# A recurrent attention kernel with a gated FFN: steps by halves of heads, the last eight tokens of each segment projected in advance, and an FFN at 512 tokens

## The chip, the cores and the metric

The kernel runs on one NeuronCore of a Trainium2 chip. The metric is the device time of one execution, in microseconds (us). The fast runs of one kernel lie within about 1% of each other. An experiment was timed against the kernel before on the same chip, in the same rounds. Over the different rounds the median of the kernel before went from 3629 to 3643 us, so differences of a few tens of microseconds between runs of different rounds are uncertain.

## The reference, cut to what matters

```python
# x: [2048, 1024]; 32 heads of 128; segments of 32 tokens; 8 memory tokens; FFN width 3584
mem = mem0                                          # [8, 1024]
for s in range(64):                                 # 64 steps, each needs the one before
    h = concatenate([mem, x[32*s : 32*s+32]])       # 40 rows
    q, k, v = h @ Wq, h @ Wk, h @ Wv                # each weight 1024 x 4096, bf16: 8 MB
    p = softmax(mask(q @ k.T * 128**-0.5))          # the memory rows see all 40, the others are causal
    o = (p @ v) @ Wo                                # Wo: 4096 x 1024, 8 MB
    mem = o[:8]
    outs.append(o[8:])
a = concatenate(outs)
b = (gelu(x @ w_gate) * (x @ w_up)) @ w_down        # FFN
g = sigmoid((x * gate_w).sum(-1, keepdims=True))
out = g * a + (1 - g) * b
```

The recurrence runs through `mem`. Each step needs all four attention weights, 32 MB together, which is more than fits in SBUF, the on-chip memory, here: about two thirds of it can stay. A step has only 40 rows to multiply, so it has little arithmetic per byte of weight.

## The kernel before

The weights are cut into 64 pieces of 512 KB ("pieces"). 41 stay in SBUF for all steps (tiles `res`). The other 23 are loaded again in every step through five buffers (tiles `ring`). SP issues these loads. The next load into a buffer is issued when PE has used the old content:

```python
streamed = [((p + 1) * NSTR) // 64 > (p * NSTR) // 64 for p in range(64)]
def load_str():
    ...
    p = str_pos[n % NSTR]
    t = ring[n % NRING]                                          # NRING = 5
    op("sp", lambda e: e.dma_start(dst(t, p), src(p)), wr=[t.r()], lane=f"ring{n % NRING}")
def consumed(s, p):
    if not streamed[p]:
        return
    ...
    load_str()
```

Semaphores are not written by hand. A helper notes for every operation what it reads and writes, and derives the waits. A transfer carries a `lane` and is asynchronous. If a write meets an earlier asynchronous write of the same region, the later one waits until the earlier one has landed:

```python
def _touch(self, op, reg, write, async_):
    ...
    if kind == "S":                       # SBUF: one key for each 64 bytes of a partition's offset
        keys = [("S", c) for c in range(reg[1] // CELL, (reg[2] + CELL - 1) // CELL)]
    else:
        keys = [reg]                      # any other tuple is its own key
    ...
    for k in keys:
        ...
        w, rd = c
        if write:
            if w is not None and (w.sem is not None or w.eng != op.eng or async_):
                deps.append(w)            # wait for the earlier writer
...
for o in ops:                             # emit(), per engine, in program order
    for s, v in o.waits:
        e.wait_ge(s, v)                   # the engine's sequencer stands here
    ins = o.fn(e)
```

An SBUF region is an offset and a length within a partition. The helper does not know which partitions are written.

In a step, 24 tokens of the segment and the 8 memory rows form one product of 32 rows. The last 8 tokens of a segment do not depend on memory. They are projected in every fourth step for four segments together (second input `xR`, which doubles the q, k and v products of that step). All heads are treated at once, so the softmax stands in series with the products:

```python
R = i == 0                                                 # i = s % 4
quad(s, "q", 0, *bq[0]); ...; quad(s, "k", 1, *bq[3])     # each quad: 8 pieces, one half of the heads
op("pe", f_sa, ...); op("pe", f_sb, ...); ...              # scores of all heads, both orientations
quad(s, "v", 0, *bv[0])
op("pe", f_d, ...)                                         # shift by the maximum
op("act", ... ACTF.Exp ...)
quad(s, "v", 1, *bv[1])
op("pe", f_den, ...)                                       # denominators
op("act", ... ACTF.Ln ...); op("dve", ...); op("act", ... ACTF.Exp ...)
op("pe", f_pva, ...)                                       # p @ v, needs all of the above
for g in range(4): ...                                     # copies to oT
for gp in range(4): ...                                    # 16 pieces of Wo, the first needs oT
...                                                        # result, transpose, new memory columns of hT
```

The FFN follows, at 256 tokens a time: w_down stays in SBUF, and the slabs of w_gate and w_up are loaded again for each of the eight groups, four slabs ahead.

## Time and profile before

| quantity | value |
|---|---|
| median of 3 runs | 3643.69 us (3643.08 to 3645.5) |
| span of the profiled run | 3637.2 us, mean granted clock 0.858 |
| one step, mean | 42.9 us |
| steps, all 64 | to about 2844 us |
| FFN | 793 us |

The first line of the profile's page gives each engine's busy time, its share of the span and its instruction count:

```profile
PE 2512.6 (69%) x44606; PEld 1401.3 (39%) x44678; DVE 800.5 (22%) x1873; ACT 565.3 (16%) x1315; POOL 115.9 (3%) x348
```

PE is the busiest engine, but 69% is an average over stages with different limits. The view by stretch separates them. Its columns are named in its first line; the stretches shown are the steps, two short stretches of one step, each just behind a softmax wait, and the FFN:

```profile
core 0: us, PE busy (x) PEld busy (x) DVE busy (x) ACT busy (x) POOL busy (x), PEclk, DMA share, GB/s
142.00:2802.00 2660.00, 1801.24 (x38522) 902.79 (x38522) 445.15 (x1023) 355.05 (x819) 96.45 (x248) 0.85 0.83 286
...
1062.00:1064.00 2.00, 2.00 (x55) 1.01 (x45) 0.78 (x3) 0.01 (x1) 0.00 (x0) 1.00 0.43 150
1074.00:1076.00 2.00, 2.00 (x56) 1.54 (x52) 0.00 (x0) 0.00 (x0) 0.00 (x0) 0.62 0.37 89
2899.00:3637.00 738.00, 609.94 (x4403) 445.16 (x4472) 322.49 (x731) 176.41 (x445) 0.00 (x0) 0.92 0.53 166
```

During the steps the DMA engines are busy for 0.83 of the time, PE for 1801 of 2660 us. In the two short stretches DMA falls to about 0.4 while PE is fully busy: PE had stood in a softmax wait just before, the ring had filled meanwhile, and nothing was left to load.

The timeline of PE shows both kinds of waiting. Columns are the start, the duration, engine and line, operation, output and inputs, shapes and count; brackets hold PE's idle time before it and what ended it:

```profile
1049.74 0.40 PE L496 MATMUL pb<-ring_90,hT_56 128*32 128x512 bf16 x4 [0.69 <-DMA ring_90<-in_A_Wq_dram]
1051.15 0.40 PE L496 MATMUL pb<-ring_91,hT_56 128*32 128x512 bf16 x4 [0.25 <-DMA ring_91<-in_A_Wk_dram]
1052.42 0.40 PE L496 MATMUL pb<-ring_92,hT_56 128*32 128x512 bf16 x4 [0.44 <-DMA ring_92<-in_A_Wk_dram]
1053.86 0.40 PE L496 MATMUL pb<-ring_93,hT_56 128*32 128x512 bf16 x4 [0.60 <-DMA ring_93<-in_A_Wk_dram]
...
1069.79 0.45 PE L692 MATMUL pb<-EA,vA 32*128 32x40 bf16 x32 [1.85 <-DVE vA L521]
...
1072.60 0.62 PE L727 MATMUL pb<-res_126,oT 128*32 128x256 bf16 x8 [2.12 <-DVE oT L710]
```

At first PE uses one streamed piece every 1.27 to 1.44 us and waits for each one: the loads bound this part. Later it waits 1.85 us for the copy of v and 2.12 us for the copies of the attention result: the serial chain bounds that part. The waits of PE over 1000 to 2000 us (total, times, longest) say the same of many steps:

```profile
PE pb L727 <- DVE oT L710: 36.1, 17, 2.1
PE pb L692 <- DVE vA L521: 33.3, 18, 1.9
PE pb L496 <- DMA xR<-xb_scr: 31.8, 6, 6.6
...
PE pb L496 <- DMA ring_90<-in_A_Wq_dram: 16.6, 16, 1.9
```

The third line is the special step that waits for `xR`.

### The profile page before, as it was taken

What the parts mean: (1) busy time and instruction counts of PE and PEld (TensorE: products, weight loads), DVE (VectorE), ACT (ScalarE), POOL (GpSimd) and SP (SyncE); (2) the same over time, 40 slices, a digit from 0 to 9 for tenths busy, and PEclk for the clock granted to TensorE, in tenths of its full rate; (3) what the DMA queues carried; (4) which work ended last, traced back from release to release, by engine and by line L of the source; (5) the groups of instructions that cost most, each with busy time, mean ns of one, the idle gap of its engine ahead of it and who ended that gap; (6) DMA issues with size and microseconds to landing.
All of it is one profiled execution on the core that took longest, in us unless ns stands there. A gap on an engine that the chain in (4) does not pass through costs nothing.

```text
span 3637.2 us, 95669 instructions
## 1 busy us (share of the span) xinstructions
PE 2512.6 (69%) x44606; PEld 1401.3 (39%) x44678; DVE 800.5 (22%) x1873; ACT 565.3 (16%) x1315; POOL 115.9 (3%) x348
## 2 busy tenths in 40 slices
PE   3667666666666666767676666766666488888887
PEld 2233333333323333333333333333332366666665
DVE  1111111111111111111111111111111144444444
ACT  2111111111111111111111111111111022222222
POOL 1000000000000000000000000000000000000000
PEclk9688888988888788878887988888888699999998
DMA  8987887888787978787887888787978655555554
GB/s 300 357 288 270 281 295 278 305 282 306 258 314 255 317 255 312 265 292 270 303 281 271 309 278 287 262 312 260 305 264 318 240 174 173 174 173 174 173 174 126
DMA packets 437038, 957.86 MB, mean 263 GB/s; under 512 B 51736, under 2 KB 178712, under 8 KB 436640
## 3 DMA queue, kind: packets, MB, share of 16 engines
q1 hardware_dynamic: 421280, 939.15, 75.1%
q10 hardware_dynamic: 15360, 12.59, 1.1%
q8 instruction: 349, 5.72, 0.6%
q14 instruction: 49, 0.40, 0.0%
HBM read 934.82 MB, written 16.78 MB: 262 GB/s over the span
## 4 chain that ended last, share of the span: by engine, by line
PE 44%; DMA 39%; DVE 7%; ACT 4%; issue 4%; SPq 1%; POOL 1%; ACTq 0%; POOLq 0%
PE pb L496 14%; PE pb L727 8%; PE pb L848 8%; PE pb L873 4%; DMA xR<-xb_scr 3%; DMA ring_91<-in_A_Wk_dram 3%; DMA ring_93<-in_A_Wk_dram 3%; DMA ring_92<-in_A_Wk_dram 3%; DMA ring_94<-in_A_Wk_dram 3%; PE pb L528 2%; DMA ring_90<-in_A_Wk_dram 2%; PE pb L733 2%; DMA ring_93<-in_A_Wq_dram 2%; DMA ring_91<-in_A_Wq_dram 2%; DMA ring_94<-in_A_Wq_dram 2%
## 5 line engine op out<-in xcount | busy, mean ns | idle before, releaser
L858 DVE SCALAR_TENSOR_TENSOR tp<-s_145,pb 128x256 f32<-128x256 f32 x224 | 94.2, 420 | 304.5 <-ACT s_145 L857 304.5
L848 PE MATMUL pb<-xT,rb_138 128*128 128x256 bf16 x896 | 124.7, 286 | 50.2 <-DMA rb_138<-in_B_w_gate_dram 50.2
L857 ACT ACTIVATE s_145<-pb 128x256 f32<-128x256 f32 x224 | 85.9, 383 | 452.8 <-PE pb L848 396.3
L848 PE MATMUL pb<-xT,rb_140 128*128 128x256 bf16 x896 | 122.6, 282 | 40.1 <-DMA rb_140<-in_B_w_gate_dram 40.1
L727 PE MATMUL pb<-res_126,oT 128*32 128x256 bf16 x512 | 42.4, 402 | 143.3 <-DVE oT L710 101.9
L848 PE MATMUL pb<-xT,rb_139 128*128 128x256 bf16 x896 | 122.0, 281 | 5.6 <-DMA rb_139<-in_B_w_up_dram 5.6
L848 PEld LDWEIGHTS pb<-xT,rb_138 128*128 128x128 bf16 x896 | 91.3, 102 | 88.5 <-DMA rb_138<-in_B_w_gate_dram 52.4
L848 PE MATMUL pb<-xT,rb_141 128*128 128x256 bf16 x896 | 120.4, 279 | 4.5 <-DMA rb_141<-in_B_w_up_dram 4.5
L675 DVE SCALAR_TENSOR_TENSOR pb<-pb,LN 128x320 f32<-128x320 f32 x64 | 31.9, 499 | 400.7 <-ACT LN L673 400.7
L848 PEld LDWEIGHTS pb<-xT,rb_140 128*128 128x128 bf16 x896 | 90.3, 101 | 77.2 <-DMA rb_140<-in_B_w_gate_dram 42.1
L861 DVE SCALAR_TENSOR_TENSOR g_147<-tp,pb 128x256 f32<-128x256 f32 x224 | 94.4, 422 | 108.9 <-ACT tp L860 108.9
L860 ACT ACTIVATE tp<-tp 128x256 f32<-128x256 f32 x224 | 93.2, 416 | 115.8 <-DVE tp L858 115.8
L692 PE MATMUL pb<-EA,vA 32*128 32x40 bf16 x2048 | 25.4, 183 | 123.8 <-DVE vA L521 88.8
L519 ACT ACTIVATE vA<-pb 128x512 bf16<-128x512 f32 x64 | 38.2, 597 | 424.1 <-PE pb L496 424.1
L848 PEld LDWEIGHTS pb<-xT,rb_139 128*128 128x128 bf16 x896 | 89.8, 101 | 20.4 <-DMA rb_139<-in_B_w_up_dram 8.0
L541 DVE COPY qT<-pb 128x1024 bf16<-128x1024 bf16 x64 | 44.3, 692 | 242.0 <-PE pb L528 242.0
L848 PEld LDWEIGHTS pb<-xT,rb_141 128*128 128x128 bf16 x896 | 89.2, 100 | 18.2 <-DMA rb_141<-in_B_w_up_dram 6.4
L541 DVE COPY kT<-pb 128x512 bf16<-128x512 bf16 (+1 forms) x112 | 51.7, 461 | 179.8 <-PE pb L528 179.8
L710 DVE CAST oT<-pb 128x320 bf16<-128x320 f32 x128 | 62.9, 492 | 121.4 <-ACT oT L708 121.4
L519 ACT ACTIVATE tok_71<-pb 128x512 bf16<-128x512 f32 x55 | 32.8, 597 | 320.0 <-PE pb L496 296.2
L873 PE MATMUL pb<-wd,GT_149 128*128 128x512 bf16 x273 | 73.2, 388 | 13.4 <-DVE GT_149 L863 11.6
L521 DVE CAST tok_72<-pb 128x512 bf16<-128x512 f32 x38 | 26.2, 690 | 251.5 <-PE pb L496 215.8
(408 smaller groups left out, 5138.2 us busy)
## 6 DMA issues: line engine op xcount, KB each, us to landing
ring_90<-in_A_Wk_dram SPq DMA_DIRECT2D x77, 512.0 KB, 6.2
ring_91<-in_A_Wk_dram SPq DMA_DIRECT2D x77, 512.0 KB, 6.4
ring_93<-in_A_Wk_dram SPq DMA_DIRECT2D x77, 512.0 KB, 6.1
ring_94<-in_A_Wk_dram SPq DMA_DIRECT2D x77, 512.0 KB, 6.3
ring_91<-in_A_Wv_dram SPq DMA_DIRECT2D x77, 512.0 KB, 6.5
ring_92<-in_A_Wv_dram SPq DMA_DIRECT2D x77, 512.0 KB, 6.4
ring_94<-in_A_Wv_dram SPq DMA_DIRECT2D x77, 512.0 KB, 6.5
ring_90<-in_A_Wv_dram SPq DMA_DIRECT2D x77, 512.0 KB, 6.5
```

The costliest lines, as they stand in the source:

```text
L496: ins = e.matmul(PB[bk][32 * g:32 * g + 32, :], lhsT=st[:, kc, :], rhs=w[:, g * 512:(g + 1) * 512], start=(kc == 0), stop=(kc == KC - 1))
L519: op("act", lambda e: e.activation(o_ap, PB[bank][:, :], ACTF.Copy), rd=[BK(bank)], wr=[reg])
L528: ins = e.transpose(PBV[bank][:, c:c + 128], t[:, j * 128:(j + 1) * 128], ident[:, :])
L541: op("dve", lambda e: e.tensor_copy(o_ap, i_ap), rd=[BK(bank)], wr=[reg])
L727: ins = e.matmul(PB[0][32 * g:32 * g + 32, 0:256], lhsT=oT[:, a, gp, 0:32], rhs=w[:, c:c + 256], start=(n == 0 and hh == 0), stop=(n == 15 ...
L733: ins = e.matmul(PB[1][32 * g:32 * g + 32, 0:256], lhsT=oTR[:, a, gp, :], rhs=w[:, c:c + 256], start=(n == 0 and hh == 0), stop=(n == 15 a ...
L848: ins = e.matmul(PB[hb][:, half * 256:(half + 1) * 256], lhsT=w[:, kc, c:c + 128], rhs=xT[:, rg * RG:(rg + 1) * RG, kc, :], start=(kc == 0 ...
L857: op("act", lambda e: e.activation(s1[:, :], hg, ACTF.Square, scale=SQ), rd=[BK(hb)], wr=[s1.r()])
L858: op("dve", lambda e: e.scalar_tensor_tensor(out=tp[:, :], in0=s1[:, :], scalar=1.0, in1=hg, op0=ALU.add, op1=ALU.mult), rd=[BK(hb), s1.r( ...
L860: op("act", lambda e: e.activation(tp[:, :], tp[:, :], ACTF.Tanh, scale=C_GELU), rd=[tp.r()], wr=[tp.r()])
L861: op("dve", lambda e: e.scalar_tensor_tensor(out=g1[:, :], in0=tp[:, :], scalar=1.0, in1=hu, op0=ALU.add, op1=ALU.mult), rd=[BK(hb), tp.r( ...
L873: ins = e.matmul(PB[4 + t * 2 + hf][:, :], lhsT=gt[:, t * 128:(t + 1) * 128], rhs=wd[:, j, hf * 512:(hf + 1) * 512], start=(j == 0), stop= ...
```

## The change

The intent: the recurrent step should be bound by its weight loads alone. For that the softmax chains of one half of the heads are set beside later products. The special steps go: the last 8 tokens of all segments are projected once, in a first stage, and each step loads what it needs of them. Smaller tiles leave room for 43 resident pieces, so 21 are streamed instead of 23. The FFN works on 512 tokens at a time with w_gate and w_up resident and w_down streamed.

The core of the diff, with cuts marked by dots:

```diff
-        xb_scr = nc.dram_tensor("xb_scr", [NT, 128, KC * 32], BF16)
+        qk_scr = nc.dram_tensor("qk_scr", [4, 128, NSEG, 128], BF16)
+        v_scr = nc.dram_tensor("v_scr", [4, NRT, 1024], BF16)
+        o_scr = nc.dram_tensor("o_scr", [128, NSEG, 256], BF16)
 ...
+        for n, (mat, u) in enumerate(QUADS):              # first stage: 512 last tokens, K=1024
+            ...                                            # q and k transposed, a head at a time
+                    if hb % 8 == 6:
+                        hh = hb // 8
+                        op("act", lambda e, st=st, m=m, hh=hh: e.dma_start(qk_scr[m, :, :, 64 * hh:64 * hh + 64], st[:, :, :]),
+                           rd=[st.r()], wr=[("D", "qk", m, hh)], lane=f"stq{hh}")
+                    if n > 0:
+                        next_x()                           # transpose a tile of x, issue the next x load on ACT
 ...
+        def load_v(s):                                     # v of the last 8 tokens of segment s
+            for g in range(4):
+                op("sp", lambda e, g=g: e.dma_start(vB[32 * g:32 * g + 8, :, :].rearrange("p a c -> p (a c)"),
+                                                    v_scr[g, NB * s:NB * s + NB, :]),
+                   rd=[("D", "v", NB * s // RB)], wr=[vB.r()], lane=f"vb{g}")
 ...
-            R = i == 0
-            ... quad(s, "q", 0, *bq[0]) ... f_sa, f_sb ... quad(s, "v", 1, *bv[1]) ... f_pva, f_pvb ...
+            on(2, start_step)                              # stores of the step before; load_h(s+1), load_qk(s+1)
+            on(8, lambda: evac(A0, tok[0], "act"))
+            ...
+            on(26, lambda: scores(0))
+            on(28, lambda: scores_T(0))
+            on(32, lambda: shift(0))
+            on(36, lambda: denom(0))
+            on(40, lambda: scores(1))
+            on(44, lambda: attend(0))
+            on(46, lambda: shift(1))
+            on(49, lambda: denom(1))
+            on(55, lambda: attend(1))
+            on(56, lambda: load_v(s + 1) if not last else None)
+            for p in range(64):
+                for f in at.get(p, ()):
+                    f()
+                proj(p, s)                                 # one piece; then load_str() if streamed
 ...
-        RG = 2                                             # FFN: 256 tokens, gate/up slabs reloaded
+        FB = min(S, 512)                                   # FFN: 512 tokens, wg and wu resident
+        ...                                                # before it: output product of all last tokens
+        for b in range(NBK):
+            ...
+            act_copy(ox[:, 0:16], ov[:, 0:16], [orT[b % 2].r()], [ox.r(0, hx)])
+            dve_copy(ox[:, 16:32], ov[:, 16:32], [orT[b % 2].r()], [ox.r(hx, 2 * hx)])
```

## The prediction

It was written from the kernel before, its profile and the diff, before anything of the change had run.

> **What bounds it now.** Three parts, read from the timeline of PE. 0 to 68 us: x is transposed. 68 to 2844 us: 64 recurrent steps, 43.4 us each on average; the plain step at 1042.1 took 38.4 us, every fourth, which also projects the last-8 tokens of four segments, about 51. 2844 to 3637: FFN, 793 us.
>
> Steps (stretch 1000 to 2000): PE busy 0.68, DMA share 0.82, 285 GB/s. The chain of waits alternates between ring loads of Wq/Wk/Wv/Wo and the serial softmax chain (about 4 us at 1058 to 1062, 5 us at 1067 to 1072, 2 us at the end). The issue list gives 1472 ring loads, 23 of 512 KB per step. Where they stream freely PE consumes one every 1.3 us (1049.7 to 1057.7), so 23 take 30 us. In the other 8 us the ring of five had filled during a softmax wait (DMA share fell to 0.37 to 0.43), or a load came late. So: loads first, softmax second, PE never.
>
> FFN: a 256-token group takes 92 us: 28 x 2.61 us of dense PE (73) plus about 11 us waiting for gate/up slabs that are reloaded each group, and a restart at a granted clock near 0.65. Entry wastes about 50 us.
>
> **What the change does.**
> - Steps: special steps vanish. Scores, shift, denominator, attention of one half stand several pieces after their inputs, so PE should hardly wait for ACT/DVE. PE work is 64 x 0.216 + 4 = 18 us, far below the loads. Smaller tiles free 6.5 KB per partition: 43 resident pieces instead of 41, 21 streamed. New small loads per step cost about 1.2 us of engine time, estimated from packets here (384 B: 22 ns, 512 B: 28 ns, 2 KB: 95 ns). Estimate: 21 x 1.33 + 1.2 + 2 disturbed = 31.3 us. The Trainium skill ("DMA: Bandwidth & Descriptors", Issuing engines are not separate DMA queues) says all queues share the 16 engines; so loads stay the bound.
> - First stage, added: six quads x 128 products x 0.216 = 166 us, 13 us of transposes, 18 us of first loads: 198 us instead of 68. PE work is not saved (222 us removed from 16 special steps, 166 + 55 added); it moves to where PE, not DMA, is the limit. The first step also loads ten Wo pieces: 47 us.
> - Output product of the last-8 tokens: 4 x 13.8 us plus 14 of loads: FFN starts 70 us after the last step.
> - FFN: 4 x (28 x 3.46 + 56 x 0.87) = 581 us dense. w_down is streamed at about 250 GB/s, below the 400 seen. 10 us of tail.
>
> Sum: 198 + 47 + 63 x 31.3 + 70 + 581 + 10 = 2878 us, say **2880**; range **2760 to 3030**. Faster by over 2%: 0.98; within: 0.01; slower: 0.01.
>
> **What would show it.** Plain step near 31 us with DMA share over 0.93 and 21 ring loads; PE's waits nearly all for ring loads, hardly any for oT, vA, LN. First stage ends near 200 us, PE busy 0.9. FFN near 581 us at granted clock about 1.0: the Trainium skill ("TensorE: Matmul & The Clock Gate", HAM oscillation) says gaps over about 3 us drop the clock, as after today's 10 us waits.
>
> **What would make it wrong.** A step above 34 us: small transfers or SP's issue order hold up ring loads, or residual softmax waits; each us is 63 us of total. 128-byte stores of last-8 q/k stall the first stage (30 to 100 us). w_down arriving late. Below 2760: loads stream at 1.28 us per piece throughout.

## More of the kernel before

The length of a step is read from the last operation of each, the transpose of the new memory rows. The view of one source line gives its shortest, median and longest duration in ns, then its first and last start:

```profile
L747 PE MATMUL pb<-ident,a_bf_60 x64: 219/229/314, 142.3 to 2801.8; 128*128 128x128 bf16 x64
```

62 steps lie between these two, so one takes (2801.8 − 142.3) / 62 = 42.9 us.

## The result, and the profile after

The kernel after takes 3471.62 us in the median of 4 runs (3461.53 to 3481.32). The kernel before, run beside it, takes 3643.39 (3631.11 to 3645.5). The ratio is 0.9535 [0.95, 0.957]. Ratios here and below are the mean time of one kernel's fast runs over that of the other's fast runs of the same rounds, so they are not quite the ratio of the medians quoted; brackets hold the 95% interval. The change gains 4.7%, which is far from the 21% predicted.

The profiled run has a span of 3479.6 us at a mean clock of 0.85. Its page begins:

```profile
PE 2584.2 (74%) x38522; PEld 1095.3 (31%) x38566; DVE 758.9 (22%) x1837; ACT 631.1 (18%) x1453; POOL 143.5 (4%) x383
```

A step is again read from the transposes of the new memory rows (two to a step now, so 126 are 63 steps):

```profile
L778 PE MATMUL pb<-ident,a_bf x126: 219/229/314, 316.3 to 2735.1; 128*128 128x128 bf16 x126
```

(2735.1 − 316.3) / 62 = 39.0 us, where the prediction had 31.3. The waits of PE over 1000 to 2000 us are now:

```profile
PE pb L701 <- DMA ring_79<-in_A_Wq_dram: 26.6, 11, 5.9
PE pb L701 <- DMA ring_80<-in_A_Wq_dram: 26.4, 14, 6.1
PE pb L701 <- DMA ring_78<-in_A_Wq_dram: 25.8, 12, 6.4
PE pb L701 <- DMA ring_81<-in_A_Wq_dram: 25.6, 11, 6.2
```

The softmax waits are gone from the top of the list, as predicted. What remains is waiting for streamed pieces, but the longest such waits are about 6 us, and an unhindered ring delivers a piece every 1.3 us. The view by stretch, with the same columns as before, shows the steps, five stretches of 2 us around the end of one step, and the FFN:

```profile
316.00:2735.00 2419.00, 1692.67 (x33604) 694.31 (x33604) 406.27 (x1303) 427.29 (x1116) 97.53 (x310) 0.81 0.84 294
...
1018.00:1020.00 2.00, 1.41 (x52) 1.40 (x52) 0.00 (x0) 0.00 (x0) 0.85 (x3) 1.00 0.96 363
...
1022.00:1024.00 2.00, 1.67 (x32) 0.63 (x24) 0.00 (x0) 0.49 (x1) 0.00 (x0) 1.00 0.05 12
1024.00:1026.00 2.00, 0.00 (x0) 0.00 (x0) 0.00 (x0) 0.11 (x1) 0.00 (x0) 0.99 0.03 8
1026.00:1028.00 2.00, 0.00 (x0) 0.00 (x0) 0.00 (x0) 0.00 (x0) 0.00 (x0) 0.50 0.64 213
1028.00:1030.00 2.00, 0.75 (x8) 0.29 (x12) 0.00 (x0) 0.00 (x0) 0.00 (x0) 0.50 0.90 289
2866.00:3479.00 613.00, 586.63 (x2672) 263.26 (x2689) 274.78 (x401) 138.95 (x226) 0.00 (x0) 0.99 0.34 119
```

Between 1022 and 1026 the 16 DMA engines do almost nothing (0.05 and 0.03), although PE runs out of weights at 1023.67. So the loads are not slow. They have not been issued. The timeline of SP's queue tells why; the second column is how long SP stood in the issue:

```profile
1016.16 0.34 SPq L340 DMA_DIRECT2D ring_78<-in_A_Wk_dram  x1
1016.55 9.16 SPq L554 DMA_DIRECT2D vB<-v_scr  x4
1025.75 0.36 SPq L340 DMA_DIRECT2D ring_79<-in_A_Wq_dram  x1
```

A ring load is issued in 0.34 us. The four small loads of `vB` hold SP for 9.16 us, and no ring load leaves in that time. The chain of waits (start, length, what was waited for) splits this up:

```profile
1016.55 5.64 DMA vB<-v_scr
...
1022.20 1.70 DMA vB<-v_scr
...
1023.91 1.52 DMA vB<-v_scr
```

The first `vB` load runs behind the ring loads that were queued ahead of it and lands after 5.64 us. The next two take 1.7 and 1.5 us on idle DMA engines. Each is issued only after the one before has landed. SP's own waits over 1000 to 2000 us (25.63 steps) show it as a total:

```profile
SPq L340 <- PE pb L701: 359.1, 280, 3.9
SPq L554 <- DMA vB<-v_scr: 191.2, 75, 7.3
```

The first line is harmless: SP waits for PE to free a buffer of a full ring. The second is 191.2 / 25.63 = 7.46 us in each step. 75 waits are about three to a step, the number of gaps between four chained loads.

The reason is in `load_v`. The four loads go to four disjoint groups of 8 partitions, but each declares that it writes the whole of `vB.r()`, and the tracker does not see partitions. So it puts a write-after-write wait between each two of them. The Trainium skill ("DMA: Bandwidth & Descriptors", Anatomy of one DMA) says that DMA engines do not wait on semaphores and that "any semaphore wait happens on the issuing sequencer before dispatch". This trace agrees: the waits stand in SP, 8.86 of the 9.16 us, and hold up every ring load that comes after.

The first stage ends late too, at 263.8 us against 198. The timeline of ACT shows one cause, an issue that took 16.57 us right after a store of q or k:

```profile
108.59 0.54 ACTq L499 DMA_DIRECT2D qk_scr<-stq_134  x1
109.16 16.57 ACTq L405 DMA_DIRECT2D px_127<-in_A_x_dram  x1
126.17 0.60 ACT L455 ACTIVATE xq_131<-pb 128x512 bf16<-128x512 bf16 x1 [19.43 <-issue]
```

That store writes 1 MB as 8192 packets of 128 bytes. ACT neither issues nor copies until the issue behind that store is through; the issue on ACT just before the store took 0.33 us.

Where the 601.6 us between the predicted 2878 and the span of 3479.6 lie:

| part | predicted | measured | difference |
|---|---|---|---|
| first stage | 198 | 263.8 | +66 |
| first step | 47 | 52.5 | +5.5 |
| 63 steps | 63 × 31.3 | 63 × 39.0 | +485 |
| output product of the last tokens | 70 | 93 | +23 |
| FFN and tail | 591 | 613 | +22 |

### The profile page after: what moved, and what is told of

Read it like the earlier page. It is cut to its first block, busy times and chain, and to the rows that moved or that the text cites. A ratio compares the mean times of both kernels' runs of the same rounds, so it can differ in the third digit from the quotient of the medians.

```text
span 3479.6 us, 84141 instructions
## 1 busy us (share of the span) xinstructions
PE 2584.2 (74%) x38522; PEld 1095.3 (31%) x38566; DVE 758.9 (22%) x1837; ACT 631.1 (18%) x1453; POOL 143.5 (4%) x383
## 4 chain that ended last, share of the span: by engine, by line
DMA 47%; PE 42%; SPq 6%; issue 3%; DVE 2%; ACTq 1%; ACT 0%
PE pb L701 13%; DMA vB<-v_scr 12%; PE pb L919 11%; PE pb L953 4%; PE pb L712 3%; DMA ring_82<-in_A_Wk_dram 3%; PE pb L486 3%; DMA ring_82<-in_A_Wo_dram 2%; DMA ring_79<-in_A_Wo_dram 2%; DMA ring_80<-in_A_Wo_dram 2%; DMA ring_80<-in_A_Wk_dram 2%; DMA ring_78<-in_A_Wo_dram 2%; SPq L788 2%; DMA ring_81<-in_A_Wo_dram 2%; DMA ring_79<-in_A_Wk_dram 2%
## 5 line engine op out<-in xcount | busy, mean ns | idle before, releaser
L568 ACT ACTIVATE tok_76<-pb 128x512 bf16<-128x512 f32 x128 | 76.4, 597 | 615.1 <-PE pb L701 615.1
L568 ACT ACTIVATE tok_77<-pb 128x512 bf16<-128x512 f32 (+1 forms) x128 | 62.8, 490 | 545.9 <-PE pb L701 545.9
L571 DVE COPY kT_69<-pb 128x512 bf16<-128x512 bf16 x64 | 27.2, 424 | 574.3 <-PE pb L585 574.3
L927 ACT ACTIVATE s_162<-pb 128x512 f32<-128x512 f32 x112 | 66.8, 596 | 326.9 <-DVE osb_164 L968 172.5
L571 DVE COPY qT_65<-pb 128x512 bf16<-128x512 bf16 x64 | 27.2, 424 | 438.2 <-PE pb L585 438.2
L571 DVE CAST oT<-pb 128x160 bf16<-128x160 f32 x256 | 71.1, 319 | 217.2 <-PE pb L682 217.2
L568 ACT ACTIVATE oT<-pb 128x160 bf16<-128x160 f32 x256 | 63.8, 301 | 248.6 <-PE pb L682 248.6
L701 PE MATMUL pb<-ring_78,hT_56 128*32 128x512 bf16 x384 | 47.7, 486 | 62.1 <-DMA ring_78<-in_A_Wq_dram 43.1
L701 PE MATMUL pb<-ring_78,hT_55 128*32 128x512 bf16 x384 | 47.1, 479 | 59.5 <-DMA ring_78<-in_A_Wk_dram 30.5
L701 PE MATMUL pb<-ring_82,hT_56 128*32 128x512 bf16 x384 | 46.9, 477 | 57.3 <-DMA ring_82<-in_A_Wq_dram 37.4
L701 PE MATMUL pb<-ring_81,hT_56 128*32 128x512 bf16 x384 | 45.2, 459 | 59.0 <-DMA ring_81<-in_A_Wq_dram 40.2
L701 PE MATMUL pb<-ring_79,hT_56 128*32 128x512 bf16 x384 | 46.8, 475 | 53.9 <-DMA ring_79<-in_A_Wq_dram 34.3
L701 PE MATMUL pb<-ring_80,hT_56 128*32 128x512 bf16 x384 | 45.5, 462 | 55.2 <-DMA ring_80<-in_A_Wq_dram 35.1
L701 PE MATMUL pb<-ring_80,hT_55 128*32 128x512 bf16 x384 | 47.6, 484 | 47.4 <-DMA ring_80<-in_A_Wq_dram 25.6
L701 PE MATMUL pb<-ring_82,hT_55 128*32 128x512 bf16 x384 | 47.4, 482 | 44.3 <-DMA ring_82<-in_A_Wq_dram 23.8
L701 PE MATMUL pb<-ring_81,hT_55 128*32 128x512 bf16 x384 | 47.4, 481 | 43.1 <-DMA ring_81<-in_A_Wq_dram 26.0
L701 PE MATMUL pb<-ring_79,hT_55 128*32 128x512 bf16 x384 | 47.4, 482 | 42.4 <-DMA ring_79<-in_A_Wq_dram 25.6
L611 DVE TENSOR_REDUCE nm_58<-pb 128x8 f32<-128x320 f32 x64 | 31.5, 492 | 197.6 <-PE pb L607 197.6
L953 PE MATMUL pb<-wd_141,GT 128*128 128x512 bf16 x299 | 70.0, 386 | 5.3 <-DMA wd_141<-in_B_w_down_dram 5.0
L953 PE MATMUL pb<-wd_140,GT 128*128 128x512 bf16 x294 | 67.9, 379 | 3.0 <-DMA wd_140<-in_B_w_down_dram 2.4
L568 ACT ACTIVATE kT_70<-pb 128x512 bf16<-128x512 bf16 x64 | 38.2, 597 | 175.3 <-PE pb L585 175.3
```

The costliest lines, as they stand in the source:

```text
L568: op("act", lambda e: e.activation(o, i, ACTF.Copy), rd=rd, wr=wr)
L571: op("dve", lambda e: e.tensor_copy(o, i), rd=rd, wr=wr)
L611: op("dve", lambda e: e.tensor_reduce(nm[u][:, :, :].rearrange("p a b -> p (a b)"), PB[SS][:, 0:320].rearrange("p (a c) -> p a c", c=LQ), ...
L701: ins = e.matmul(PB[bk][32 * g:32 * g + 32, :], lhsT=h[:, kc, :], rhs=w[:, g * 512:(g + 1) * 512], start=(kc == 0), stop=(kc == KC - 1))
L927: op("act", lambda e, hg=hg: e.activation(s1[:, :], hg, ACTF.Square, scale=SQ), rd=[BK(bg)], wr=[s1.r()])
L953: ins = e.matmul(PB[bank[2 * k + hf]][:, :], lhsT=GT[:, j, tb * 128:(tb + 1) * 128], rhs=w[:, jj, hf * 512:(hf + 1) * 512], start=(j == 0) ...
```

## The experiments

The theory: chained `vB` loads hold SP, the ring empties, and this is most of the step's excess (Theory 1). The rivals: the added small loads cost DMA time themselves, by many short packets (a packet is the unit in which the profile lists what a DMA engine moves); the ring of five is too shallow; a piece costs more than 1.33 us; a residual softmax wait. A second question is the first stage, where 128-byte stores are suspected. All kernels passed the comparison with the reference.

### v_split: the four loads no longer wait for each other

Four keys of the tracker stand for the four partition groups; the loads write one each, the consumer reads all four. Nothing else changes. The loads keep their waits for the consumer of the step before.

```diff
+        VQ = [("V", g) for g in range(4)]
+        op("pool", lambda e: e.memset(vB[:], 0.0), wr=[vB.r()] + VQ)
 ...
-                   rd=[("D", "v", NB * s // RB)], wr=[vB.r()], lane=f"vb{g}")
+                   rd=[("D", "v", NB * s // RB)], wr=[VQ[g]], lane=f"vb{g}")
 ...
-            op("pe", f, rd=[vA[u].r(), vB.r(), EE[u].r()], wr=[BK(b) for b in bo])
+            op("pe", f, rd=[vA[u].r(), vB.r(), EE[u].r()] + VQ, wr=[BK(b) for b in bo])
```

> The kernel after, with the four loads of vB (8 rows of each 32-row group) tracked as four separate regions instead of one, so that SP no longer waits for one of them to land before it issues the next. Bytes, packets and order are unchanged. Theory 1 (SP stands in that chain 7.5 us of each step, so no ring load is issued and the ring of five runs dry): the step falls from 39.2 us to 31 to 33, the total from 3472 to about 3000 (2950 to 3070), DMA share in the steps from 0.84 to over 0.93. Rival 2 (the step is long because the new small transfers slow the ring loads on the 16 DMA engines): the transfers are the same, so the step stays above 38 us and the total above 3400.

Measured: 3096.93 us (3088.85 to 3100.46), ratio to the kernel before 0.8529 [0.8495, 0.8563], on a chip where that took 3629.04. The step is 33.05 us, (2360.6 − 311.8) / 62 by the first line below. The total lies 27 us above the range that was expected. The stretch of its steps and its timeline of SP's queue are to be read like those of the kernel after:

```profile
L780 PE MATMUL pb<-ident,a_bf x126: 219/229/314, 311.8 to 2360.6; 128*128 128x128 bf16 x126
...
312.00:2361.00 2049.00, 1543.23 (x33606) 661.52 (x33604) 406.46 (x1303) 427.42 (x1116) 97.52 (x310) 0.91 0.99 347
```

```profile
1035.39 0.34 SPq L340 DMA_DIRECT2D ring<-in_A_Wk_dram  x1
1035.78 1.34 SPq L556 DMA_DIRECT2D vB<-v_scr  x4
1037.23 2.18 SPq L340 DMA_DIRECT2D ring<-in_A_Wq_dram  x3
```

The same four loads of the same bytes are issued in 1.34 us instead of 9.16, and the DMA share of the steps rises from 0.84 to 0.99. The chain costs (39.01 − 33.05) × 63 = 375 us; by the two ratios, (0.9535 − 0.8529) × 3643 = 366 us. The loads themselves are still there, so their packets are not what these 375 us are. The mean clock of the steps goes from 0.81 to 0.91 as the gaps go.

### v_pool: the same chain on a queue with nothing behind it

Here the false waits stay. The issuer changes, and with it the place: POOL issues the loads at the start of the step that uses them, and no longer SP near the end of the step before.

```diff
-        def load_v(s):
+        def load_v(s, eng="sp"):
 ...
-                op("sp", lambda e, g=g: e.dma_start(vB[32 * g:32 * g + 8, :, :].rearrange("p a c -> p (a c)"),
+                op(eng, lambda e, g=g: e.dma_start(vB[32 * g:32 * g + 8, :, :].rearrange("p a c -> p (a c)"),
 ...
+                if s > 0:
+                    load_v(s, "pool")                      # in start_step, after put_rest(s)
 ...
-            on(56, lambda: load_v(s + 1) if not last else None)
```

> The kernel after, with the same four chained loads of vB, each still waiting for the one before, but issued from POOL's queue just after the step's POOL copies, so that POOL stands in the chain and not SP. Theory 1 in its strict form (what costs is that SP is blocked): about as fast as v_split, within 60 us of it. Rival 3 (what costs is that the chained vB lands late, or the small transfers themselves): stays near 3470.

Measured: 3105.18 us, ratio 0.8556 [0.8524, 0.8589], step 33.06, the same as v_split. Its line of the transposes, and one of POOL's waits over 1000 to 2000 us:

```profile
L779 PE MATMUL pb<-ident,a_bf x126: 219/229/314, 317.2 to 2366.7; 128*128 128x128 bf16 x126
...
POOL vB L554 <- DMA vB<-v_scr: 435.9, 86, 7.3
```

POOL stands in the chain for 436 of 1000 us, more than twice what SP stood, and it costs nothing, since nothing urgent is queued behind it. So in this kernel the chain is dear on the queue that feeds the bottleneck, and free on one that does not. The Trainium skill ("DMA: Bandwidth & Descriptors", Issuing engines are not separate DMA queues) says that all issuers end on the same 16 engines. The step of 33.06 against 33.05 us fits that, but does not test it, since only four small loads changed their issuer.

### v_two: a dose between

Two keys for two pairs of loads, so that one false wait remains within each pair. The edit is that of v_split with

```diff
+        VQ = [("V", g) for g in range(2)]
 ...
+                   rd=[("D", "v", NB * s // RB)], wr=[VQ[g // 2]], lane=f"vb{g}")
```

> The kernel after with the four vB loads tracked as two regions: loads 1 and 2 are chained, 3 and 4 are chained, so SP waits for landings twice instead of three times (load 3 does not wait). A dose between after (39.0 us a step) and v_split (33.05). In the trace of after the first wait of a chain is about 5.5 us (it lands behind the queued ring loads), the next ones 1.5 us each. If the loss is the time SP stands still: standing falls from about 8.7 us to about 7, step about 37.5, total about 3380. If the loss came from the number of waits, it would fall by a third to a half: step 35 to 36, total about 3250.

Measured: 3390.22 us, ratio 0.9313 [0.9288, 0.9339], step 37.69. SP's waits over 1000 to 2000 us:

```profile
SPq L556 <- DMA vB<-v_scr: 166.5, 54, 6.0
```

166.5 us in 26.5 steps are 6.28 us a step. Three doses stand in order: 7.46 us of standing and a step of 39.01, 6.28 and 37.69, none and 33.05. Counted from none, a microsecond of standing costs 0.74 to 0.80 us of step; the rest may be covered by the pieces that are already in the ring, which was not tested. Between the two chained kernels alone it is 1.32 / 1.18 = 1.1, so the doses do not lie on a line. Two waits instead of three help little, because the first wait is the long one: it lies behind all ring loads queued before it.

### no_qkr and no_loads: what the small loads cost in themselves

Both start from v_split: no_qkr loads q and k of the last tokens only for the first step; no_loads also leaves away the loads of v and of x after the first steps. Their outputs are wrong, which doesn't matter for the times.

```diff
 # no_qkr
-                    load_qk(s + 1)
 # no_loads: as well
-                if not last:
+                if s == 0:                                 # guards load_h(s + 1)
 ...
-            on(56, lambda: load_v(s + 1) if not last else None)
+            on(56, lambda: None)
```

> v_split without the load of the last-8 q/k in each step after the first (512 packets of 256 bytes): a wrong result on purpose, to price that load. If a transfer costs only its own packet time (32 packets of 18 ns on each engine = 0.57 us), the step falls from 33.05 to 32.5 and the total to about 3060. If it also slows the weight packets beside it (4 KB packets took 290 to 335 ns instead of 160 in the two microseconds in which it ran), the step falls by 1.3 to 2 us, to about 31.4, and the total to about 2990.

> v_split without any of the three small loads of a step after the first steps (last-8 q/k, the segment's x, vB): a wrong result on purpose, to price them all. Counted as their own packets they are 0.57 + 0.22 + 0.18 = 0.97 us on each engine; with the mark-up that no_qkr showed (0.77 us for 0.57) 1.3 us: step 31.7 to 32.1, total 3010 to 3035. If small transfers explain all that lies between 33.05 us and 21 pieces at the marginal 1.36 us of nstr23 (4.5 us), the step falls to 30 or less, total under 2910; then what is left must be the stores or the slow weight packets.

Measured: no_qkr 3043.31 us, ratio 0.8374 [0.8354, 0.8394], step 32.28; no_loads 2998.27 us, ratio 0.8242 [0.8222, 0.8263], step 31.33, where 31.7 to 32.1 had been expected:

```profile
L779 PE MATMUL pb<-ident,a_bf x126: 219/229/314, 312.7 to 2255.2; 128*128 128x128 bf16 x126
```

All small loads of a step together so cost 33.05 − 31.33 = 1.72 us. Their own packets take 0.97 us of each DMA engine in the trace of v_split, so they cost more than they occupy. The mean 4 KB packet of the ring loads fell from 184 to 179 ns when they were gone, which over the 120 such packets of a step on each engine is about 0.6 us and may be most of the rest. That is arithmetic on two traces and was not tested by itself. The rival "small loads", priced without the chain, is thus worth 1.7 us a step. The prediction had counted 1.2 of that, so 0.5 of a step's 7.7 us excess is left to it.

One warning on correctness: the comparison passed these two kernels, although each is wrong by construction. It therefore says little about the attention path. That v_split is right rests on the disjoint partitions and on the race check, which it passed.

### nstr23: two more streamed pieces

From v_split, two pieces fewer are resident: two of Wq, Wk or Wv, whose loads move in packets of 4 KB.

```diff
-        NRES = (top - cur[0]) // PIECE
+        NRES = (top - cur[0]) // PIECE - 2
```

> v_split with two pieces fewer resident, so 23 pieces of 512 KB are streamed per step instead of 21. Theory (the step of v_split is set by the ring loads, each worth its mean packet time: 8 packets of 4 KB of 185 ns on each of 16 engines = 1.48 us): the step grows by 2.96 us to 36.0, the total by about 186 to 3283. The size used in the prediction, 1.33 us a piece, gives +168, step 35.7. Rival (PE or its waits set the step): grows by less than 1 us a step.

Measured: 3271.25 us, ratio 0.8987 [0.896, 0.9014], step 35.77, with a DMA share of 0.99:

```profile
L780 PE MATMUL pb<-ident,a_bf x126: 219/230/314, 320.4 to 2538.4; 128*128 128x128 bf16 x126
```

One more piece costs (35.77 − 33.05) / 2 = 1.36 us. So the loads do bound the step once the chain is gone, and the prediction's 1.33 us a piece was nearly right. The mean packet of 4 KB, 184 ns in the trace of v_split with eight of them to a piece on each engine, would have given 1.47 us, which is too much. That mean holds slow packets (the median is 159 ns); why they do not grow in proportion was not tested. The six pieces of Wo that a step streams move in packets of 2 KB and were not priced.

### ring4: one buffer fewer

From v_split, with the freed buffer holding a resident piece.

```diff
-    NRING = 5
+    NRING = 4
 ...
-        s1 = al("s1", [128, FB], FP32)
+        s1 = al("s1", [128, FB], FP32, at=low)              # so that the FFN's tiles still fit
```

> v_split with a ring of four slots instead of five and one more piece resident: 20 streamed per step. If the fifth slot is not needed once SP is not held up, the step falls by 1.48 us to 31.6 and the total to about 3005, DMA share still 0.98 or more. If the ring's depth matters, DMA share in the steps falls below 0.95 and the step stays at 33 or more.

Measured: 3197.89 us, ratio 0.878 [0.875, 0.8811], step 34.55, although it streams one piece less. The stretch of its steps:

```profile
325.00:2467.00 2142.00, 1580.12 (x33605) 667.53 (x33604) 405.75 (x1302) 429.88 (x1116) 98.43 (x310) 0.90 0.93 317
```

The hope that four buffers would do was wrong. DMA share falls from 0.99 to 0.93. With one piece less and nothing lost it would have been 33.05 − 1.36 = 31.7 us, so the missing buffer costs about 2.9 us a step. Five buffers reach 0.99 without the chain, so their number alone is not what held the kernel after. Whether a deeper ring would have hidden part of the chain was not tried.

### qk_rows and v_split_qk: the 128-byte stores of the first stage

The scratch of q and k is laid out so that each store has 128 rows of 8 KB; the loads in the steps become 1024 rows of 128 bytes instead of 512 of 256.

```diff
-        qk_scr = nc.dram_tensor("qk_scr", [4, 128, NSEG, 128], BF16)
+        qk_scr = nc.dram_tensor("qk_scr", [4, 2, 128, NSEG, 64], BF16)
 ...
-                        op("act", ... e.dma_start(qk_scr[m, :, :, 64 * hh:64 * hh + 64], st[:, :, :]),
+                        op("act", ... e.dma_start(qk_scr[m, hh, :, :, :], st[:, :, :]),
 ...
-            op("sp", lambda e: e.dma_start(qkr[:, :, :], qk_scr[:, :, s, :].rearrange("m p c -> p m c")),
+            op("sp", lambda e: e.dma_start(qkr[:, :, :].rearrange("p m (h c) -> p (m h) c", h=2), qk_scr[:, :, :, s, :].rearrange("m h p c -> p (m h) c")),
```

qk_rows has it on the kernel after, v_split_qk on v_split.

> The kernel after, with the scratch tensor of last-8 q/k laid out so that each of the eight first-stage stores writes 128 rows of 8 KB instead of 8192 rows of 128 bytes; the load in each step then reads 1024 pieces of 128 bytes instead of 512 of 256. Theory (ACT is held while it issues the transfer behind such a store, up to 17 us, and PE then waits for x tiles and for PSUM to be emptied): the first stage ends near 205 us instead of 262, the total falls by 45 to 65 us, to about 3415; steps change by less than 0.5 us. Rival (the first stage is held by its x loads or by the DMA engines as a whole): it shortens by less than 15 us.

> Both edits together. If the two causes lie in separate stages they add up: the total is that of v_split less 45 to 65 us, about 2945.

Measured: qk_rows 3427.35 us, ratio 0.9451 [0.9406, 0.9496], which is 44 us less than the kernel after (31 us by the two ratios). Its first stage ends at 228.6 us instead of 263.8. Its timeline of ACT shows the issue behind the store to be short now:

```profile
93.95 0.35 ACTq L499 DMA_DIRECT2D qk_scr<-stq  x1
94.33 0.45 ACTq L405 DMA_DIRECT2D px<-in_A_x_dram  x1
```

So the 16.57 us were due to the 8192 small packets. About 35 of the 66 us are shown to be theirs; 205 us had been expected for the end of the stage, so the rest has another cause. v_split_qk takes 3077.88 us, ratio 0.8468 [0.8426, 0.851]: only 19 us less than v_split. Its first stage is again 34 us shorter, but its step is 33.31 instead of 33.05 us, which gives 16 us back over the steps. A 128-byte packet takes 13.0 ns (v_split_qk) and a 256-byte packet 17.9 (v_split); with 64 and 32 of them on each engine in a step this is 0.83 against 0.57 us, just the 0.26 that the step grew. qk_rows shows no such growth over the kernel after (38.71 against 39.01 us). The likely reason is that its DMA engines have idle time in each step; that is argued and not tested.

### best and best2: the parts put together

best is v_split with one store for all 16 heads (rows of 256 bytes on both sides), x loaded two tiles ahead, and the copies for the second block of the output product issued before the first product.

```diff
-        stq = [al(f"stq{i}", [128, NSEG, 64]) for i in range(2)]
+        stq = al("stq", [128, NSEG, 128])
 ...
-                    if hb % 8 == 6:
+                    if hb == 14:
+                        op("act", lambda e, st=st, m=m: e.dma_start(qk_scr[m, :, :, :], st[:, :, :]),
 ...
-        x_tiles = [load_x(xf[0:128, :], 128, "act")]
+        x_tiles = [load_x(xf[T * 128:(T + 1) * 128, :], 128, "act") for T in range(2)]
 ...
+        put_ox(0)
+        for b in range(NBK):
+            if b + 1 < NBK:
+                put_ox(b + 1)
```

> v_split with three repairs outside the steps: one store of 128 rows of 16 KB for each q/k half instead of two of 8192 pieces of 128 bytes (the load in the step keeps its 256-byte pieces), x tiles loaded two ahead instead of one, and in the output product of the last-8 tokens the rearranging copies for the next block ahead of the emptying of PSUM for this one. First stage ends near 205 us instead of 262, the entry to the FFN takes about 82 us instead of 93, steps stay at 33.05: total about 3030, 55 to 75 below v_split. If the x loads still queue behind resident loads, the first stage ends at 225 to 235 and the gain is 35 to 50.

Measured: 3043.96 us (3034.67 to 3049.55), ratio 0.837 [0.8347, 0.8394]. The first stage ends at 235.7 us, not near 205 as hoped, the step is 32.96, and the output product of the last tokens takes 75.5 us instead of 93. In the kernel after PE had waited 28.9 us there for the copies that gather the last tokens; in best it waits 17.9, all of it for the first of them.

best2 spreads the loads of resident pieces in the first stage, to see whether their burst delays the x tiles:

```diff
-    def load_res(p):
+    def load_res(p, after=()):
 ...
+                            some([mm])                     # one resident load for each pair of heads
```

> best with the resident loads of the quad after next issued one per head pair instead of in one burst of 3 MB at the end of each quad, so that x tiles do not queue behind them. PE waited 21.5 us for x tiles in the first stage of best: most of that goes. First stage ends near 215 us instead of 236, total about 3025, steps unchanged at 33.

Measured: 3040.76 us (3030.75 to 3063.55), ratio 0.8369 [0.8327, 0.841], the same as best. The first stage ends at 228.2 us in its trace, where 215 had been expected, and PE still waits 19.7 us for x tiles, so the burst is not their main cause. They are issued on ACT's queue behind the store of q or k, which takes 12.4 us; that this is the cause is argued and not shown.

Both beat the kernel after by about 12% and the one before by 16%.

## Why the prediction was wrong

It said 2880 us with a range of 2760 to 3030. The result was 3471.62, faster as said, but by less than a quarter of the gain.

**The step that failed.** It is "Estimate: 21 x 1.33 + 1.2 + 2 disturbed = 31.3 us", with "so loads stay the bound". It takes for granted that a ring load leaves as soon as its buffer is free. It does not: SP stood 7.46 us a step in the issue of four loads that the dependency tracker had chained. Of the 601.6 us by which the profiled run is longer, 375 are this chain (v_split takes it away). The prediction did name "SP's issue order" among what could make it wrong, but only as a risk. The cause could have been read from the diff: four asynchronous writes that declare one region, and a tracker that waits for an earlier asynchronous writer.

**Terms of that sum that were mis-sized.** Without the chain the step is 33.05, not 31.3. A piece costs 1.36 against 1.33 us (nstr23); small loads cost 1.72 against 1.2 (no_loads); what is left is 33.05 − 21 × 1.36 − 1.72 = 2.8 against 2 (the three predicted numbers add up to 31.1). Over 63 steps the 1.75 us make 110 us. What the 2.8 us consist of is only in part known. In the trace of v_split stores, instruction fetches and semaphore writes take about 1 us of each engine in a step, and the packets of the 21 pieces 30.8 us, which is 2.2 more than 21 × 1.36. Part of that may already be in the 1.72, of which only 0.97 are the small loads' own packets. Why these packets are slower than the price of one more piece stays open.

**First stage, 66 us.** The prediction named "128-byte stores … stall the first stage (30 to 100 us)" as a risk and did not count it. About 35 us are shown to be theirs (qk_rows). The rest goes with 21.7 us of waits for x tiles that v_split_qk still shows and the prediction had not counted; their cause is open. The 12.4 us for the first weights are within the 18 us of first loads that it had.

**Output product and FFN, 45 us.** The prediction had 4 × 13.8 = 55 us of products and 14 of loads. The products took about 64 us (93 − 28.9). The 28.9 us are the waits for the gathering copies; the first of them, 18.7 us, contains the landing of what is copied (10.1 us), so it is the copies, and the issues that stood ahead of that load, that had not been counted. In best this part is 17.5 us shorter, 11 us of it in these waits. In the FFN the mechanism was right: PE is busy for 586.6 of 613 us at a clock of 0.99. The prediction's dense 581 us and 10 us of tail lack 7.9 us of waits for GT, 9.7 for w_down, and the rest of the tail.

**What held.** The softmax waits vanished. 21 pieces are streamed. The steps are bound by loads once SP is free, with a DMA share of 0.99 (over 0.93 was said). The clock was rightly tied to gaps: in the kernel after it goes from 0.99 to 0.50 at 1026 us, in the gap that the chain makes, and the mean of the steps rises from 0.81 to 0.91 in v_split. The timeline of PE has this gap and a shorter one just after it; two stretches show the clock in the shorter:

```profile
1023.28 0.39 PE L701 MATMUL pb<-res_89,hT_56 128*32 128x512 bf16 x4
1029.25 0.62 PE L701 MATMUL pb<-ring_79,hT_56 128*32 128x512 bf16 x4 [5.58 <-DMA ring_79<-in_A_Wq_dram]
...
1036.57 0.62 PE L701 MATMUL pb<-ring_82,hT_56 128*32 128x512 bf16 x4 [2.76 <-DMA ring_82<-in_A_Wk_dram]
```

```profile
1035.00:1036.00 1.00, 0.00 (x0) 0.00 (x0) 0.00 (x0) 0.00 (x0) 0.00 (x0) 1.00 0.89 283
1036.00:1037.00 1.00, 0.43 (x8) 0.14 (x8) 0.00 (x0) 0.00 (x0) 0.00 (x0) 0.60 1.01 381
```

A group of four products before the first gap takes 0.39 us, one behind it 0.62 us, at half the clock. The Trainium skill ("TensorE: Matmul & The Clock Gate", HAM oscillation) puts the gap that does this at more than about 3.4 us, which the prediction rounded to 3. In the first gap the clock fell about 2.3 us after the last product had ended (1023.67 to 1026), and the second, in which it fell again, is 2.76 us long in all. So shorter gaps are enough here, and the measurement decides.

**Where the expected gain went.** It was turned into a new wait on the queue that feeds the bottleneck. v_split alone, 3096.93 us, lies 67 us above the predicted range; best, 3043.96 us, lies 14 us above it.

## What to carry to other kernels

Before trusting a sum of transfer times, list what each issuing queue does in order and ask of each issue what it waits for: a wait there delays everything behind it, however small the transfer. If waits are derived by a helper, look at what its regions cannot express (here partitions); several loads into one tile may be chained for no reason. When the DMA engines are idle and the consumer waits for data, look at the issuer and not at the bandwidth.

## What the Trainium skill lacked or had wrong

- "DMA: Bandwidth & Descriptors", Issuing engines are not separate DMA queues: it says the time of issuing "is usually small relative to the DMA itself". Most issues shown here agree (0.33 to 0.54 us), but an issue behind a store of 8192 packets of 128 bytes held ACT for 16.57 us, and 0.45 us when that store had 128 rows of 8 KB. The section does not warn of this.
- The same page, Why small descriptors are slow: it gives 27% overhead for 256 bytes by the first of two mechanisms and no time for the second. In the trace of v_split a 256-byte packet takes 17.9 ns, where its share of a 4 KB packet (median 159 ns) would be 9.9 ns, so about 45% of its time is overhead in all; 512 bytes take 27.8 ns there, and 128 bytes 13.0 in v_split_qk.
- The same page: it does not say that a mean of packet times misleads for a loaded engine. The 4 KB packets have a median of 159 and a mean of 184 ns; the measured cost of one more 512 KB piece, 1.36 us, lies below what the mean gives (1.47).
- The same page: it does not say what small transfers cost beside large ones. 0.97 us of their own packets cost 1.72 us of a step.
- The same page: it does not say how many loads to keep in flight. Five buffers of 512 KB gave a DMA share of 0.99, four gave 0.93.
- "TensorE: Matmul & The Clock Gate", HAM oscillation: gaps over about 3.4 us are said to lower the clock; here it fell in a gap of 2.76 us, and within about 2.3 us of the last product in one of 5.58 us.
- The chain of waits through one in-order issuer is in "DMA: Bandwidth & Descriptors" as one sentence (Anatomy of one DMA); what it can cost is not: 7.46 us of standing at SP cost 5.96 us of each step.
